# Attention and a two-level expert layer: three moves in the order of the last phases

## The chip, the cores and the metric

The kernel runs on one core of one Trainium2 chip. Its time is the device time in microseconds; three runs of the kernel before took 474.42, 475.54 and 475.85 us, with a median of 475.54. A profiled execution, from which all durations below are taken, spans 474.8 us from the first to the last instruction.

## The reference

Two computations follow each other. The first is attention with 16 query heads that share one key and value head, for 8 batches of 384 tokens with head dimension 64. The second is a hierarchical mixture of experts: each of the 3072 tokens takes the best of 4 groups, then the best of that group's 4 experts, and goes through that expert's two matrices only.

```python
scores = scale * q @ k.T                    # per batch and head
attn = softmax(scores) ; x = attn @ v       # x: 3072 tokens x 1024
g_idx = argmax(x @ w_group)                 # 4 groups, softmax weight g_w
e_idx = argmax(x @ w_expert[g_idx])         # 4 experts in it, softmax weight e_w
h = maximum(x @ w1[g_idx, e_idx], 0)
out = (g_w * e_w) * (h @ w2[g_idx, e_idx])
```

## The kernel before

**Blocks.** A block `p` is 128 queries of one batch with all 16 heads; there are 24 of them, three to a batch (`b, st = divmod(p, 3)`). Each has six pieces `j` of 64 keys. `scores` multiplies queries by keys into a PSUM tile and ScalarE takes its exponential (lines 245 to 254); `pre_add` and `fold_keys` sum the exponentials on VectorE; `values` accumulates the output of the block before in one PSUM tile with a single buffer; `weigh` (line 295) divides by the sums on VectorE and lets GpSimd make the bf16 copy `xbf`.

**Order.** The schedule is written out by hand: each engine executes its instructions in program order, and the loop of lines 549 to 617 sets it. TensorE computes the first three scores of block `p`, then in turn values of block `p - 1` and further scores of block `p`.

**Expert units.** Tokens of one batch mostly choose the same expert. From the first 128 tokens of a batch the kernel counts which expert is chosen most (`choose_a`, `counts`, `choose_b`), reads its number into a register and loads that expert's weights through GpSimd's DMA queue. The batch is then computed with it in 14 units: eight first-layer units of eight matmuls (line 416) with a ReLU on ScalarE, and six second-layer units of eight matmuls (line 424) with a scaled copy on ScalarE. `fill(n)` (line 460) issues the next `n` units. The blocks from 4 on run four or five units each at their end; block 4 (`ST + 1`) has three more, ahead of its `pre_add`. All of these short-lived PSUM results go round one pool of three buffers (`side`, line 76).

**Leftovers.** Tokens that did not choose the counted expert are handled at the end. `counts` sums the one-hot choices over tokens with a matmul of ones: line 342 for the first 128 tokens of a batch, line 344 for the whole batch, whose result goes to `gate_c`. For the last two batches one call holds both: batch 7's first tokens and all of batch 6. Its copy in SBUF, tag `cnt1`, has one buffer. `early_pair` (line 511) reads the counts of all batches, finds one pair of batch and expert that is left over, and loads its number into a register of GpSimd, VectorE and SyncE (line 531); `leftover_w1`, called when 92 units have run, loads the pair's first matrix, and `leftover_w2`, at 98 units, the second. After the last block, the tail packs up to 32 tokens of this pair (`rank_of`, `pick`), transposes their batch's activations (`xe`, line 690), and runs them through the two matrices (`px`, `ph`, `py`), ending in one indirect store (line 723).

**The rare case.** If more is left over, or if the softmax without a subtracted maximum could overflow, a block behind a branch runs (line 774). `bound_a` takes the maxima of the squared query and key norms on VectorE, `bound_b` transposes them on TensorE and compares; `rarei` adds the two conditions, and `values_load` at line 683 reads it into a register of every engine, which the branch tests. With these inputs the block does not run.

## Time and profile before

| what | value |
|---|---|
| time, median of three runs | 475.54 us |
| profiled span | 474.8 us |
| TensorE busy (matmuls) | 459.5 us, 97% |
| VectorE busy | 304.7 us, 64% |
| ScalarE busy | 246.8 us, 52% |
| mean granted clock of TensorE | 0.992 |
| data moved by DMA | 74.52 MB, mean 157 GB/s |

In the profile PE is TensorE's matmuls and PEld its weight loads, which overlap them; DVE is VectorE, ACT ScalarE, POOL GpSimd, SP SyncE. A name with a small q, such as PEq, is an engine's sequencer[...]. Brackets behind an instruction give its engine's idle time just before it and what ended it. The granted clock is TensorE's, as a share of full speed. Idle time counts only where the engine that waits holds up the end.

### The profile page before, as it was taken

To read this page: it belongs to the slowest core of one execution; us is meant where nothing else is said; L and a number is where in the kernel's file an instruction comes from. 1 tells how busy PE (TensorE), PEld (TensorE's weight loads), DVE (VectorE), ACT (ScalarE), POOL (GpSimd) and SP (SyncE) were. 2 spreads that over 40 slices of the span, in tenths; PEclk is the share of its full clock that TensorE was granted. 3 is DMA by queue.
4 is the path that set the end of the run, shared out by engine and by line. 5 is a ranking of instruction groups with operands and counts; after the bars stand their busy time and mean duration, and the time that the engine had idled before them with its cause. 6 is when DMAs were issued, how large, how long until landed. Compare 5 with 4: busy or idle time off the path is not lost. (4 is left out here: it accounts for less than half of the span.)

```text
span 474.8 us, 9339 instructions
## 1 busy us (share of the span) xinstructions
PE 459.5 (97%) x3791; PEld 196.8 (41%) x3807; DVE 304.7 (64%) x483; ACT 246.8 (52%) x359; POOL 60.4 (13%) x83
## 2 busy tenths in 40 slices
PE   8999999999999999999999999999999999999892
PEld 6333434433443344433434334433444334434541
DVE  3998868685695477683694685873687755943200
ACT  2966546546456545645465465565465463613231
POOL 1004003000130003000030001200030000340000
PEclk9999999999999999999999999999999999999898
DMA  8788996978499493967699491987849611899961
GB/s 162 91 132 123 216 211 99 218 170 206 73 172 227 167 157 48 204 146 209 116 138 213 159 166 52 193 159 207 159 66 207 179 60 46 134 213 275 266 177 60
DMA packets 152162, 74.52 MB, mean 157 GB/s; under 512 B 120216, under 2 KB 138652, under 8 KB 152112
## 3 DMA queue, kind: packets, MB, share of 16 engines
q0 software_dynamic: 28416, 37.84, 46.7%
q1 hardware_dynamic: 122896, 35.81, 31.9%
q8 instruction: 32, 0.52, 0.4%
q10 hardware_dynamic: 800, 0.20, 0.2%
q14 instruction: 18, 0.15, 0.1%
HBM read 92.62 MB, written 19.01 MB: 235 GB/s over the span
## 5 line engine op out<-in xcount | busy, mean ns | idle before, releaser
L253 ACT ACTIVATE pt<-s 128x1024 f32<-128x1024 f32 x144 | 142.8, 1026 | 63.5 <-PE s L251 61.1
L251 PE MATMUL s<-qT,kT 64*64 64x512 f32 x1152 | 144.3, 597 | 0.3 <-ACT qT L229 0.2
L290 PE MATMUL o<-pt,v 64*64 64x512 f32 x1152 | 141.0, 590 | 0.0
L261 DVE TENSOR_TENSOR presum<-presum,pt 128x1024 f32<-128x1024 f32 x96 | 116.6, 1215 | 14.7 <-ACT pt L253 8.9
L416 PE MATMUL hps<-xbf,w 128*128 128x384 bf16 x512 | 91.3, 330 | 3.0 <-DVE rarei L682 1.8
L424 PE MATMUL yps<-w,hT 128*128 128x512 bf16 x368 | 84.9, 379 | 0.8
L290 PEld LDWEIGHTS o<-pt,v 64*64 64x64 f32 x1152 | 43.4, 133 | 76.6 <-issue 76.5
L259 DVE TENSOR_TENSOR presum<-pt 128x1024 f32<-128x1024 f32 x24 | 29.1, 1211 | 65.6 <-ACT pt L253 64.9
L416 PEld LDWEIGHTS <-w 128*128 128x128 bf16 x512 | 48.8, 100 | 47.6 <-issue 19.0
L425 ACT ACTIVATE y<-yps,gsel 128x512 f32<-128x512 f32 x48 | 33.0, 687 | 67.3 <-PE yps L424 63.7
L251 PEld LDWEIGHTS s<-qT,kT 64*64 64x64 f32 x1152 | 39.0, 133 | 65.6 <-issue 52.7
L417 ACT ACTIVATE hT<-hps 128x384 bf16<-128x384 f32 x64 | 31.2, 488 | 61.4 <-PE hps L416 55.4
L302 POOL CAST xbf<-xT 128x1024 bf16<-128x1024 f32 x24 | 25.0, 1041 | 299.0 <-DVE xT L301 299.0
L424 PEld LDWEIGHTS <-hT 128*128 128x128 bf16 x384 | 36.5, 98 | 50.3 <-issue 8.5
L145 POOL DMA_DIRECT2D w<-in_moe_w_dram x36 | 24.8, 708 | 68.9 <-issue 43.2
L301 DVE TENSOR_TENSOR xT<-o,rinv 128x1024 f32<-128x1024 f32 x24 | 29.2, 1215 | 4.2 <-PE o L290 4.2
L280 DVE STREAM_TRANSPOSE rinv<-rc 128x1024 f32<-128x1024 f32 x24 | 29.9, 1246 | 0.8
L265 DVE TRANSPOSE_TENSOR_REDUCE fold<-presum 128x32 f32<-128x1024 f32 x24 | 29.6, 1232 | 0.0
L368 DVE COPY L<-lps 128x20 f32<-128x20 f32 (+1 forms) x16 | 3.0, 186 | 34.5 <-PE lps L321 34.5
L243 DVE STREAM_TRANSPOSE qT<-qraw 128x1024 f32<-128x1024 f32 x20 | 24.5, 1225 | 0.6
L209 ACT ACTIVATE qraw<-qraw 128x1024 f32<-128x1024 f32 x21 | 22.0, 1049 | 0.0
L273 PEld LDWEIGHTS sm<-fold,sel 64*64 64x64 f32 x192 | 7.2, 133 | 13.0 <-issue 13.0
(146 smaller groups left out, 167.3 us busy)
## 6 DMA issues: line engine op xcount, KB each, us to landing
w<-in_moe_w_dram POOLq DMA_DIRECT2D x36, 512.0 KB, 10.0
w<-in_moe_w_dram POOLq DMA_DIRECT2D x9, 2048.0 KB, 22.1
out_dram<-y SPq DMA_DIRECT2D x24, 512.0 KB, 3.5
qraw<-in_q_dram SPq DMA_DIRECT2D x56, 192.0 KB, 3.8
x_bf<-xbf SPq DMA_DIRECT2D x8, 768.0 KB, 4.4
v<-in_v_dram SPq DMA_DIRECT2D x16, 96.0 KB, 2.9
k<-in_k_dram SPq DMA_DIRECT2D x28, 48.0 KB, 2.7
qn<-in_q_dram SPq DMA_DIRECT2D x4, 256.0 KB, 4.5
```

The lines of the kernel that those rows point to most:

```text
L251: nc.tensor.matmul(out=ps[64 * c:64 * c + 64, a, :], lhsT=kT[b][r, j * D:(j + 1) * D], rhs=qT[p][r, c * CW:(c + 1) * CW], start=True, stop ...
L253: nc.scalar.activation(out=t[:], in_=ps[:], func=ACTF.Exp, scale=scale)
L259: nc.vector.tensor_add(out=presum[p][:], in0=pt[p, 0][:], in1=pt[p, 1][:])
L261: nc.vector.tensor_add(out=presum[p][:], in0=presum[p][:], in1=pt[p, j][:])
L265: nc.vector.tensor_reduce(out=fold[p][:], in_=presum[p][:].rearrange("p a (n i) -> p (a n) i", i=32), axis=AX, op=OP.add, apply_transpose= ...
L280: nc.vector.transpose(out=t[:].rearrange("p (b i) -> p b i", i=32), in_=rc[:].rearrange("p c b -> p (c b)").unsqueeze(2).to_broadcast([P, ...
L290: nc.tensor.matmul(out=o_ps[p][64 * a:64 * a + 64, c, :], lhsT=v_sb[b][r, j, :], rhs=pt[p, j][r, a, :], start=(j == 0), stop=(j == KB - 1))
L301: nc.vector.tensor_mul(out=xT[b][:, :, ts], in0=o_ps[p][:].rearrange("p c (h n) -> p (c h) n", n=P), in1=rinv[p][:].rearrange("p (h n) -> ...
L416: nc.tensor.matmul(out=ps[:, 0:S], lhsT=w1[:, ko, fc * P:(fc + 1) * P], rhs=xb[:, ko, :], start=(ko == 0), stop=(ko == KO - 1))
L417: nc.scalar.activation(out=state["h"][:, fc, :], in_=ps[:, 0:S], func=ACTF.Relu)
L424: nc.tensor.matmul(out=ps[:], lhsT=state["h"][:, fo, st * P:(st + 1) * P], rhs=w2[:, fo, nh * CW:(nh + 1) * CW], start=(fo == 0), stop=(fo ...
L425: nc.scalar.activation(out=y, in_=ps[:], func=ACTF.Copy, scale=gs_of()[:, st:st + 1])
```

## The change

Four things are altered. The register load of `rare` goes from directly behind `rarei` to a place in front of the last expert unit. `bound_a` goes in front of the units of the last block and `bound_b` behind them, where before they stood behind its second and third unit. The counts of batch 6 leave block 22 for the first unit of block 23, `early_pair` follows them there, and `cnt1` gets a second buffer so that the counts of batch 7's first tokens are kept meanwhile. The three additional units of block 4 go from behind its third scores to behind its fourth, which the first values of block 3 precede.

```diff
 def counts(now, full):
-        t = pool.tile([P, n], FP32, tag="cnt1", bufs=1, name="cnt1")
+        t = pool.tile([P, n], FP32, tag="cnt1", bufs=2, name="cnt1")
...
         if jobs:
             jobs.pop(0)()
-        if p == ST + 1:
-            fill(3)
         for j in (1, 2):
             pre_add(p, j)
         for j in range(KB):
...
             if jobs:
                 jobs.pop(0)()
+            if p == ST + 1 and j == 0:
+                fill(3)
...
             n = 5 if p in FIVES else 4
             steps = {}
+            if p == NP - 1:
+                bound_a()
             if st == 2:
                 steps = {0 if b == 1 else 1: lambda: counts(None, b - 1)}
                 if p == NP - 1:
-                    steps = {1: bound_a, 2: bound_b}
+                    steps = {0: lambda: (counts(None, b - 1), early_pair()), n - 1: bound_b}
             if st == 1:
                 gate_a_, gate_b_ = jobs_gates(b)
-                steps = {n - 3: gate_a_, n - 2: gate_b_, n - 1: lambda: counts(b, b - 1 if b == B - 1 else None)}
+                steps = {n - 3: gate_a_, n - 2: gate_b_, n - 1: lambda: counts(b, None)}
             for i in range(n):
                 fill(1)
                 if i in steps:
                     steps[i]()
-        if p == NP - 2:
-            early_pair()
...
     nc.vector.tensor_copy(out=rarei[:], in_=raref[:, 0:1])
-    rare = nc.values_load(rarei[0:1, 0:1], min_val=0, max_val=2, skip_runtime_bounds_check_because="a sum of two comparisons")
     fill(2)
...
         fill(1)
-    while begun[0] < B or units:
-        fill(1)
+    fill(len(units) - 1)
+    rare = nc.values_load(rarei[0:1, 0:1], min_val=0, max_val=2, skip_runtime_bounds_check_because="a sum of two comparisons")
+    fill(1)
     px = side([P, KO, CAP], FP32, "px")
```

## The prediction

> **What bounds the kernel now.** I read the page first, then TensorE's waits alone, then the order of time around the three places that the diff touches, and last the granted clock microsecond by microsecond.

> The page gives busy shares and instruction counts by engine; the second line is the total of the costliest group of first-layer expert matmuls, with the idle time ahead of it.

> ```profile
> PE 459.5 (97%) x3791; PEld 196.8 (41%) x3807; DVE 304.7 (64%) x483; ACT 246.8 (52%) x359; POOL 60.4 (13%) x83
> ...
> L416 PE MATMUL hps<-xbf,w 128*128 128x384 bf16 x512 | 91.3, 330 | 3.0 <-DVE rarei L682 1.8
> ```

> TensorE is busy 97% of 474.8 us: a microsecond of its waiting is a microsecond of the kernel. The page's chain holds only the final indirect store, so it can't show this; TensorE's own list of waits can (engine, line, who was waited for, total, times, longest):

> ```profile
> PE hps L416 <- DVE rarei L682: 1.8, 1, 1.8
> ...
> PE pq L498 <- DVE sq L492: 0.7, 1, 0.7
> PE hps L416 <- POOL xbf L302: 0.6, 1, 0.6
> ...
> PE cps L344 <- DVE ohe L382: 0.5, 1, 0.5
> ```

> Each wait belongs to an edit: `rarei` to the register load, `sq` to the bound's transpose, `xbf` to block 4's units, `ohe` to the counts that the diff pulls apart. In order of time (start, length, engine and line, idle before it):

> ```profile
> 54.31 3.90 PE L416 MATMUL hps<-xbf,w 128*128 128x384 bf16 x23 [0.62 <-POOL xbf L302]
> ...
> 401.55 0.17 PE L342 MATMUL cps<-ohe,ones_bf 128*128 128x16 bf16 x1
> 402.19 0.18 PE L344 MATMUL cps<-ohe,ones_bf 128*128 128x48 bf16 x1 [0.46 <-DVE ohe L382]
> 402.30 2.81 PE L251 MATMUL s<-qT,kT 64*64 64x512 f32 x24
> ...
> 417.62 0.38 PE L498 MATMUL pq<-ident,sq 128*1 128x128 f32 x2 [0.66 <-DVE sq L492]
> ...
> 440.47 0.73 PE L667 MATMUL pg<-gi,pick 128*128 128x2 f32 x6
> 442.98 4.44 PE L416 MATMUL hps<-xbf,w 128*128 128x384 bf16 x16 [1.78 <-DVE rarei L682]
> ```

> The last line shows more than its wait: sixteen matmuls take 4.44 us, where sixteen take 2.76 at 437.88. The clock says why (stretch, length, busy time and count of PE, PEld, DVE, ACT, POOL, then granted clock, DMA share, GB/s):

> ```profile
> 443.00:444.00 1.00, 1.00 (x5) 0.58 (x5) 0.00 (x0) 0.00 (x0) 0.00 (x0) 0.71 1.08 329
> 444.00:445.00 1.00, 1.00 (x5) 0.44 (x3) 0.00 (x0) 0.00 (x0) 0.00 (x0) 0.50 1.22 221
> 445.00:446.00 1.00, 1.00 (x4) 0.44 (x3) 0.00 (x0) 0.49 (x1) 0.00 (x0) 0.50 1.25 211
> ```

> After the wait TensorE runs about 3 us at half clock. The wait is paid twice.

> [...] TensorE's sequencer passed line 667's semaphore instruction at 439.2, its weights loaded at 440.31; VectorE's register load of line 531 began at 406.6 beside the operation of line 530 (406.60 to 406.83). [...] the 768 KB of `xe` took 8.5 us from issue to landing, the eight stores of the same size 4.4 in the median.

> **The change part by part.** Sums are made from start to start against the profiled span of 474.8 us, then carried to the median of 475.54, 0.74 above it.

> *1. Block 4's three units, behind its fourth scores.* The scores start at 50.93; the same 24 f32 matmuls ahead of units elsewhere take 2.69 (410.19 to 412.88), so the units could start at 53.62 and start at 54.31: 0.69 lost to the xbf cast, which ends at 53.21 + 1.04 = 54.25. Moved, the units stand behind eight value and eight score matmuls (0.86 each) and start at 55.3, past the cast. The values write the output accumulator, free when line 301 ends (51.94 + 1.22 = 53.16); the fourth scores need the first scores' buffer, read by 53.0; each unit needs the exponential of two scores earlier, the third that of the fourth scores (about 56.5) at 57.9. The three ReLUs now follow the fourth exponential on ScalarE, with no DMA in them. No wait in exchange: gain 0.69, bounds 0.3 and 0.7.

> *2. Counts of block 22, `early_pair`, and the second cnt1 buffer.* The first count still runs at 401.55, but the second (line 344) no longer stands between it and the next scores: 402.30 - 401.55 = 0.75 becomes 0.11, as in block 4 (73.63 to 73.74). There the 24 scores then took 2.84 to the first values, against 2.63 here (402.30 to 404.93), because one waits for the count copy behind a ReLU; I charge that 0.21. Gain 0.43. The moved count costs 0.03 in block 23 (85.85 to 85.88); its `ohe` is long ready. The buffer costs 256 bytes a partition and no time; it lets `seen` outlive the next count. `early_pair` and its three register loads (0.48 SP, 0.55 DVE, 0.29 POOL) move. SP: nothing stands behind its load between 406 and block 7's x store at 427.20. POOL: the cast at 416.32 now goes ahead of its load.

> *3. bound_a ahead of the units, bound_b behind them.* Block 23's start of units to its `sm` takes 412.88 to 419.22 = 6.34. Without waiting: four units at 1.30 (449.00 less 447.70), two transposes 0.21 (417.62 to 417.83), 0.11 of changeover and 0.03 for the count: 5.55. Gain 0.79, if `sq` is ready. With `early_pair` gone from its front, VectorE starts this block's sums near 404.3, not 407.25, and is then paced by exponentials; I get fold done at 415.1, `sq` at 415.4, and TensorE's transposes at 417.2. Behind it VectorE runs gate_c (1.1), `early_pair` (2.3), its load, and bound_b (0.9): until about 420.1, then rc and rinv until 421.7. The last values end near 422.9, so weigh isn't delayed. The transpose's PSUM buffer is free by 420, wanted at 424.6. Leftover w1 now needs that register: issue near 419.3 against 419.60 now.

> *4. The register load in front of the last unit.* TensorE gets no `rarei` wait: line 667 starts at 440.47, six such f32 matmuls need 0.58 (399.67 to 400.25), so the units start at 441.05 relative to today's clock, not 442.98: 1.93. Half clock: the two units take 447.25 - 442.98 = 4.27 against 2.60: 1.67. Together 3.60. At the new place TensorE's load (486 ns here) is bounded by 0 and 0.49; the value is ready 15 us earlier, and the sequencer was seen 1.1 us ahead, so I take 0. The other four loads (0.30 SP, 0.46 ACT, 0.31 POOL, 0.33 DVE): ACT has about 1 us idle between evacuations, VectorE is idle before px, POOL before its final store, and SP's last store is issued only when its evacuation ends.

> Sum: 0.69 + 0.43 + 0.79 + 3.60 = 5.5; span 469.3, median 475.54 - 5.5 = 470.0.

> **What an earlier TensorE may run into.** Last w1 piece: issued near 421.6, 25.1 us, landing 446.7, wanted at 464.13 - 5.5 = 458.6. Leftover w2: 437.51 + 19.9 = 457.4, wanted at 460.8. Both hold even if the DMA backlog keeps them where they are. Tightest is `xe`: issued at 434.60, landed at 443.1, first transposed at 447.09. All this moves 1.9 earlier by parts 1 to 3, but the transpose another 3.6: 441.6 against a landing at 441.2. Margin 0.4.

> **The rivals.**
> - The half clock is no stable cost: if the runs that make the median don't pay it, or another place pays it after the change, 1.67 falls away: 471.7. For: [...] a spread of 1.4 us in three runs. Against: nothing else in the last 100 us idles TensorE over 0.7 us before the end.
> - `xe` becomes the new wait by about 1 us: 471.0. For: the margin of 0.4 and a saturated DMA (share above 1 until 455). Against: `xe` keeps its neighbours, as its stores move with it.
> - TensorE's load stalls at its new place: 470.5. Against: the sequencer's lead.
> - Parts 1 to 3 give nothing: 471.9. Against: three waits with one named cause each.
> - Slower: `xe` lands far later than TensorE wants it. A wait over about 1.8 us also brings back 1.67 of half clock, so the gain is gone when `xe` lands at 441.6 + 5.5 - 1.67 = 445.4, a transfer of 12.7 us instead of 8.5. With a landing at 448: 475.54 - 5.5 + 6.4 + 1.7 = 478.1. Against: no transfer through SP's queue in this stretch took over 8.5.

> **How the numbers follow.** Mine 0.60 (alone 469.3 to 470.8), clock 0.14, `xe` 0.13, load 0.05, nothing from parts 1 to 3 0.02, gain just cancelled 0.02, slower 0.04. A difference under 0.3% (1.4 us) can't be told from none. Faster 0.94, same 0.02, slower 0.04. The range 468.9 to 472.2 takes in all the cases that end faster, and 0.4 below my own for charges that don't come (0.21) and spread.

> **What would show it.** Right: no waits of TensorE on `rarei`, `sq`, `xbf`, or on `ohe` at line 344; granted clock 1.00 through the tail; two units after line 667 in 2.6 us; no gap over 0.1 ahead of the last unit's eight matmuls. Wrong: a wait ahead of line 690 with no compute engine to name; a clock of 0.50 before the last matmul; a gap of about half a microsecond at the last unit; `pq` still waiting for `sq`, which would mean VectorE's sums were not paced as I have it.

## The result, and the profile after

The changed kernel takes 470.57 us (median of four runs, 469.97 to 471.02), the kernel before 475.7 (four runs). The ratio is 0.9893 with an interval of 0.9867 to 0.992: 5.1 us, or 1.1%, faster. The profiled span is 468.4 us, 1.6 below that execution's own time of 469.97.

The page, engines and the same group of expert matmuls as before:

```profile
PE 457.0 (98%) x3791; PEld 195.5 (42%) x3807; DVE 304.6 (65%) x483; ACT 246.9 (53%) x360; POOL 60.4 (13%) x83
...
L416 PE MATMUL hps<-xbf,w 128*128 128x384 bf16 x512 | 89.5, 326 | 0.6 <-ACT hT L417 0.6
```

The number of matmuls is the same, but they are busy for 2.5 us less, 1.8 of it in this group. Nearly all of the 1.8 is the half clock, which was booked as work: sixteen matmuls took 4.44 us before and take 2.76 now. TensorE's list of waits:

```profile
PE warm L152 <- DVE one L158: 1.3, 1, 1.3
PE hps L416 <- ACT hT L417: 0.6, 1, 0.6
PE ph L707 <- DVE xc L701: 0.5, 1, 0.5
PE phT L712 <- ACT hg L709: 0.5, 1, 0.5
PE py L719 <- DVEq L774: 0.4, 1, 0.4
PE s L251 <- ACT qT L229: 0.2, 1, 0.2
```

All four waits that the edits addressed are gone and no new one has come; what is left was there before. In order of time, TensorE at the edited places (start, length, count):

```profile
50.43 2.75 PE L251 MATMUL s<-qT,kT 64*64 64x512 f32 x24
...
54.83 4.08 PE L416 MATMUL hps<-xbf,w 128*128 128x384 bf16 x24
58.84 1.09 PE L290 MATMUL o<-pt,v 64*64 64x512 f32 x8
...
400.37 0.17 PE L342 MATMUL cps<-ohe,ones_bf 128*128 128x16 bf16 x1
400.47 3.02 PE L251 MATMUL s<-qT,kT 64*64 64x512 f32 x24
403.31 1.04 PE L290 MATMUL o<-pt,v 64*64 64x512 f32 x8
...
411.27 1.47 PE L416 MATMUL hps<-xbf,w 128*128 128x384 bf16 x8
...
416.50 0.38 PE L498 MATMUL pq<-ident,sq 128*1 128x128 f32 x2
416.82 0.30 PE L273 MATMUL sm<-fold,sel 64*64 64x16 f32 x8
...
438.06 0.73 PE L666 MATMUL pg<-gi,pick 128*128 128x2 f32 x6
438.65 2.76 PE L416 MATMUL hps<-xbf,w 128*128 128x384 bf16 x16
441.25 0.61 PE L688 MATMUL pb<-ident_bf,xe 128*128 128x128 bf16 x8
...
460.33 1.06 PE L719 MATMUL py<-w,hc 128*32 128x256 bf16 x32 [0.38 <-DVEq L774]
```

At the edited places no bracket names a releaser any more. The points of the profile before that the next table needs:

```profile
60.06 1.04 PE L290 MATMUL o<-pt,v 64*64 64x512 f32 x8
...
404.93 0.61 PE L290 MATMUL o<-pt,v 64*64 64x512 f32 x4
...
412.88 4.07 PE L416 MATMUL hps<-xbf,w 128*128 128x384 bf16 x24
...
419.22 0.30 PE L273 MATMUL sm<-fold,sel 64*64 64x16 f32 x8
...
447.25 0.61 PE L690 MATMUL pb<-ident_bf,xe 128*128 128x128 bf16 x8
...
466.34 1.06 PE L720 MATMUL py<-w,hc 128*32 128x256 bf16 x32 [0.38 <-DVEq L775]
```

The profile after is 0.5 us ahead before any edit (block 4's scores at 50.43 instead of 50.93), so I compare distances inside each profile:

| distance | before | after | gain | forecast |
|---|---|---|---|---|
| block 4, first scores to second values | 9.13 | 8.41 | 0.72 | 0.69 |
| the count at the end of block 22 to the first values in block 23 | 3.38 | 2.94 | 0.44 | 0.43 |
| block 23, units to `sm` | 6.34 | 5.55 | 0.79 | 0.79 |
| line 667 (666) to the first transpose of `xe` | 6.78 | 3.19 | 3.59 | 3.60 |
| that transpose to `py` | 19.09 | 19.08 | 0.01 | 0 |

The sum is 5.5. The two spans, 474.8 and 468.4, differ by 6.4: the rest is the 0.5 us ahead of any edit and 0.4 behind `py`, which starts 8.46 us before the end of the profile before and 8.07 before the end of the one after. The register load itself, at its new place (engine queue, minimum, median, maximum in ns, start):

```profile
L694 PEldq TENSOR_LOAD <-rarei x1: 487/487/487, 451.3 to 451.3; - x1
```

It takes 487 ns at 451.3, while the last unit, for which it stands in the program, starts near 455.1 (`px` at 456.85 less one unit of 1.73). TensorE's sequencer is 3.8 us ahead of its array there, and the load costs no time.

### The profile page after: what moved, and what is told of

It is laid out like the page before. It is cut to its first block, busy times and chain, and to the rows that moved or that the text cites. A ratio compares the mean times of both kernels' runs of the same rounds, so it can differ in the third digit from the quotient of the medians.

```text
span 468.4 us, 9356 instructions
## 1 busy us (share of the span) xinstructions
PE 457.0 (98%) x3791; PEld 195.5 (42%) x3807; DVE 304.6 (65%) x483; ACT 246.9 (53%) x360; POOL 60.4 (13%) x83
## 5 line engine op out<-in xcount | busy, mean ns | idle before, releaser
L251 PE MATMUL s<-qT,kT 64*64 64x512 f32 x1152 | 144.6, 597 | 0.3 <-ACT qT L229 0.2
L416 PE MATMUL hps<-xbf,w 128*128 128x384 bf16 x512 | 89.5, 326 | 0.6 <-ACT hT L417 0.6
L416 PEld LDWEIGHTS <-w 128*128 128x128 bf16 x512 | 48.0, 99 | 44.1 <-issue 14.8
L251 PEld LDWEIGHTS s<-qT,kT 64*64 64x64 f32 x1152 | 38.9, 133 | 65.5 <-issue 52.6
L302 POOL CAST xbf<-xT 128x1024 bf16<-128x1024 f32 x24 | 25.0, 1041 | 294.7 <-DVE xT L301 294.7
```

Source lines behind the costliest of these rows:

```text
L251: nc.tensor.matmul(out=ps[64 * c:64 * c + 64, a, :], lhsT=kT[b][r, j * D:(j + 1) * D], rhs=qT[p][r, c * CW:(c + 1) * CW], start=True, stop ...
L416: nc.tensor.matmul(out=ps[:, 0:S], lhsT=w1[:, ko, fc * P:(fc + 1) * P], rhs=xb[:, ko, :], start=(ko == 0), stop=(ko == KO - 1))
```

## The experiments

### One part at a time

The register load alone:

```diff
-    rare = nc.values_load(rarei[0:1, 0:1], ...)
     fill(2)
...
-    while begun[0] < B or units:
-        fill(1)
+    fill(len(units) - 1)
+    rare = nc.values_load(rarei[0:1, 0:1], ...)
+    fill(1)
```

> The kernel before, with the register load of the rare case alone moved to the front of the last unit. My account: TensorE's wait on rarei (1.93 us from start to start) and the half clock behind it (1.67) both go, so line 667 to the first transpose takes about 3.2 us instead of 6.8, and the time falls by 3.6 us (475.7 to about 472.1). Rival, the half clock comes from something else in the tail (the DMA peak, the narrow f32 matmuls): the wait goes, a stretch at clock 0.50 stays, the fall is 1.9 us (473.8). Rival, the load stalls TensorE at its new place: a gap of 0.5 us ahead of the last unit, the fall 3.1 us.

Measured: 472.36 us, ratio 0.9942 (0.9926 to 0.9959). Line 667 at 439.93 to the first transpose at 443.12 is 3.19 us, the clock is 1.00 up to the last matmul, and no gap precedes the last unit. In the trace the first account holds and both rivals fall. The time fell less than the 3.6 us forecast: the medians lie 3.3 apart, and the ratio stands for 2.8 (2.0 to 3.5).

Block 4's units alone:

```diff
-        if p == ST + 1:
-            fill(3)
...
+            if p == ST + 1 and j == 0:
+                fill(3)
```

> The kernel before, with block 4's three units alone moved behind its fourth scores. My account: the wait on xbf goes and nothing takes its place; from block 4's first scores (start) to its second values is 8.4 us instead of 9.1, and all that follows is 0.7 us earlier; in the time that is 0.15%, below what the runs tell apart, so the trace decides. Rival, something later takes the 0.7 us back (a DMA or a buffer): block 22 starts no earlier after block 4's start than before.

Measured: 475.43 us, ratio 1.0003 (0.9985 to 1.0021), which tells nothing, as expected. In the trace first scores to second values take 8.41 us (51.07 to 59.48). Block 22's count comes 349.95 us after those scores (401.02), where it was 350.62 (401.55 less 50.93): the 0.7 us are still there 350 us later.

The counts, `early_pair` and the bound alone (the change with the two other edits undone):

> The changed kernel with block 4's units and the register load put back where they were before: only the counts, early_pair and the bound's two halves are moved. My account: the waits on ohe and sq go, block 22's first count to the first values takes 2.9 us instead of 3.4, block 23's units 5.55 instead of 6.34, together 1.2 us (475.7 to 474.5); the wait on rarei and the half clock stay at about 1.9 and 1.7 us. Rival, the later early_pair gives it back as a wait in the last block's weigh or the leftover weights: no fall, and a new wait of TensorE in the tail.

Measured: 473.69 us, ratio 0.9968 (0.9955 to 0.9981). The first count to the values takes 2.94 us (400.98 to 403.92), block 23's units 5.54 (411.88 to 417.42), and of the waits that the edits address only those on `xbf` and `rarei` are left. Half clock follows the latter as before (sixteen matmuls in 4.30 us). VectorE's later `early_pair` costs nothing. The medians lie 1.9 us apart, more than the 1.2 expected, but the half clock seems to be in fewer executions here, which the table below takes up.

### Where the half clock comes from

The load moved by one unit only:

```diff
-    rare = nc.values_load(rarei[0:1, 0:1], ...)
-    fill(2)
+    fill(1)
+    rare = nc.values_load(rarei[0:1, 0:1], ...)
+    fill(1)
```

> The kernel before, with the register load moved by one unit only, between the two units that followed it. My account, the half clock comes from the length of the idle stretch: one unit fills 1.3 us of the wait, some 0.6 us of idle time stays in front of the second unit, and the clock stays at 1.00; the fall is 1.93 - 0.6 + 1.67 = 3.0 us (475.7 to 472.7). Rival, any wait of TensorE's sequencer on the register load brings the half clock: 0.50 for some 3 us behind the shorter wait, the fall only 1.3 us (474.4).

Measured: 472.77 us, ratio 0.9954 (0.9939 to 0.9969). TensorE's two units behind line 667:

```profile
440.83 1.46 PE L416 MATMUL hps<-xbf,w 128*128 128x384 bf16 x8
442.75 1.46 PE L416 MATMUL hps<-xbf,w 128*128 128x384 bf16 x8 [0.46 <-PE hps L416]
```

The gap is 442.75 - 440.83 - 1.30 = 0.62 us, the second unit runs at full clock, and the medians lie 2.9 us apart. In the trace, moving the load past a single unit leaves 0.62 of the 3.59 us that the whole move brings, so it brings four fifths. It also shows the load's price where it isn't hidden: 0.48 of the 0.62 (the load takes 484 ns, from 442.2 on).

But the times of the kernel before fell into two groups. Over all experiments (the last included, so some more than the expectations below speak of), 88 of 128 executions had a mean clock of 0.994 or less and a median of 475.98 us, the other 40 had 0.996 or 0.997 and 473.91. The half clock is not in every execution. To see what decides, I put waits of several lengths and kinds into the tail. First the late `xe` in the changed kernel, which is also the prediction's slower rival at a small dose:

```diff
-    nc.sync.dma_start(out=xe[:]..., in_=xb_dram[...])
...
     fill(2)
+    nc.sync.dma_start(out=xe[:]..., in_=xb_dram[...])
     pg = side([P, CW], FP32, "pg")
```

> The changed kernel, with the load of xe issued behind the output store that it precedes there, some 3.2 us later (435.4 instead of 432.2). It tests the rival of the prediction (xe as the new wait) and where the half clock comes from: this wait has no register load in it. My account: xe lands at 443.5 to 444.4, TensorE wants it at 441.1, so it waits 2.4 to 3.3 us ahead of the first transpose, and in most runs half clock follows for 3.4 us, another 1.5 us or so: 470.6 becomes 474 to 475.5[...]. Rival, the half clock belongs to the register load or to what is near it: the wait only, clock 1.00 behind it, 473 to 474. Rival, xe had slack enough: no change.

Measured: 473.28 us, ratio 0.9961 (0.9949 to 0.9973). `xe` was issued at 435.8 and took 8.3 us; TensorE waits 2.59 us ahead of line 688 (2.75 from start to start):

```profile
PE pb L688 <- DMA xe<-x_bf: 2.6, 1, 2.6
...
444.00:445.00 1.00, 0.82 (x11) 0.69 (x12) 0.16 (x1) 0.00 (x0) 0.00 (x0) 1.00 1.23 210
445.00:446.00 1.00, 1.00 (x9) 0.61 (x8) 0.53 (x1) 0.00 (x0) 0.00 (x0) 1.00 1.17 214
```

(The first line is from the waits, the others from the table by stretches: clock third from the right.) So `xe` was indeed the next thing to bind, but the longer wait has clock 1.00 behind it, and only five of 22 executions form a slower group (473.91 to 474.68). The account by length alone missed here.

Two differences to the wait on `rarei` were tried apart: that one is a register load, and it follows the six narrow matmuls of line 667, of two columns each. A wait by data at its old place, without a register load (one narrow matmul that needs a chain of VectorE copies; its result is unused), in the changed kernel:

```diff
     nc.vector.tensor_copy(out=rarei[:], in_=raref[:, 0:1])
...
+    nc.vector.tensor_copy(out=hold[:, 0:2], in_=gc[:])
+    nc.vector.tensor_copy(out=hold[:, 2:4], in_=hold[:, 0:2])
...
+    nc.vector.tensor_copy(out=holdb[:], in_=hold[:, 2:4])
...
+    nc.tensor.matmul(out=ph_[:, 0:2], lhsT=ones_bf[:], rhs=holdb[:], start=True, stop=True)
     fill(2)
```

> The changed kernel, with a wait of about 1.9 us put back where the register load stood, but without a register load: one narrow matmul (its result is not used) that needs the result of three VectorE copies behind rarei. It asks why the longer wait of the late xe (2.75 us) brought half clock in few runs. Account A, a TensorE stalled in its sequencer on a register load[...] counts as idle[...]: clock 1.00 behind the wait in nearly all runs, one group near 470.6 + 1.9 = 472.5. Account B, the narrow matmuls of line 667 ahead of the wait count as idle with it, whatever the wait is for: half clock in about two runs of three, as with the kernel before, two groups near 472.5 and 474.4.

Measured: 472.65 us, five executions, none with half clock. And the register load one unit later, behind dense matmuls, with small copies ahead of `rarei`, in the kernel before:

```diff
...
+    nc.vector.tensor_copy(out=hold[:, 0:1], in_=raref[:, 0:1])
+    for i in range(6):
+        nc.vector.tensor_copy(out=hold[:, i + 1:i + 2], in_=hold[:, i:i + 1])
...
-    nc.vector.tensor_copy(out=rarei[:], in_=raref[:, 0:1])
+    nc.vector.tensor_copy(out=rarei[:], in_=hold[:, 6:7])
+    fill(1)
     rare = nc.values_load(rarei[0:1, 0:1], ...)
-    fill(2)
+    fill(1)
```

> The kernel before, with its register load one unit later (as in the run with the load moved by one unit) and seven small VectorE copies of 0.18 us ahead of rarei, so that TensorE waits the same 1.9 us on the register load, but behind eight dense matmuls instead of behind the narrow ones of line 667. Account A (a stall on the register load is what counts as idle): half clock in about two runs of three, two groups near 473.9 and 476, as with the kernel before. Account B (the narrow matmuls count): half clock in few runs, one group near 474.

Measured: 474.31 us, seven executions in one group. Neither the register load nor the narrow matmuls alone brought it in these twelve executions. Both were then lengthened (`range(10)` for the load, five middle copies for the data wait):

> The register load behind one dense unit as in the run before, with four more copies ahead of rarei: the wait is about 2.5 us instead of 1.8, as long as the narrow matmuls and the wait together in the kernel before (2.51). Account C: time with no matmul queued and time of the narrow matmuls add up[...]: two runs of three, two groups near 475.0 and 476.7. Account D: the register load brings half clock only directly behind the narrow matmuls: one group near 475.0, clock 1.00 behind the wait.

> The matmul that waits by data behind the narrow matmuls of line 667, with four more copies ahead of it: the wait is about 2.5 us instead of 1.8, narrow matmuls and wait together 3.2 us. Account C or D[...]: clock 1.00 in nearly all runs, one group near 473.3. Account E: any wait counts, only the length decides and the shorter one fell just under it: half clock in most runs, 475.

Measured: 475.22 us for the load, five of 14 executions in a slower group (476.18 to 476.39); 474.38 us for the data wait, 13 of 15 with a mean clock of 0.993 or less, and half clock in the profiled one:

```profile
441.40 0.18 PE L689 MATMUL hold_ps<-holdb,ones_bf 128*128 128x2 bf16 x1 [2.58 <-DVE holdb L687]
441.44 4.44 PE L416 MATMUL hps<-xbf,w 128*128 128x384 bf16 x16
```

Sixteen matmuls in 4.44 us, the very figure of the kernel before, behind a wait without any register load. The shorter data wait once more, and one a step longer:

> The same kernel as the shorter data wait behind the narrow matmuls (1.9 us, with them 2.5), for more executions: five showed no half clock, where the register load with a stretch as long shows it in 79 of 116 executions of the kernel before. If the kind of wait decides at this length: none or nearly none again, one group near 472.5. If it was chance: half clock in a third or more, a second group near 474.3.

> The same with one copy more: the wait is about 2.1 us, with the narrow matmuls 2.7. If the length decides, between the none of five at 2.5 and the most of fifteen at 3.3: a quarter to two thirds of the executions at half clock, groups near 472.8 and 474.5.

Measured: 472.77 us, with half clock in one or two of six executions (473.45 at clock 0.993, perhaps 473.1 at 0.994), of which the profiled one is one; and 473.54 us, four of seven (473.54 to 473.82).

The traces point to what decides. In the profile before, the clock falls at 443.42, and it falls again when TensorE has finished and the last store is under way:

```profile
470.00:471.00 1.00, 0.00 (x0) 0.00 (x0) 0.00 (x0) 0.00 (x0) 0.00 (x0) 0.86 0.21 54
```

| what TensorE does | wait, start to start | most in one window | half clock in that profile | executions with mean clock of 0.993 or less |
|---|---|---|---|---|
| load one unit later, behind dense matmuls | 0.62 | 1.20 | no | 1 of 15 |
| data (`xe`) behind dense | 2.75 | 1.38 | no | 8 of 22 |
| load behind dense, longest | 2.54 | 1.61 | no | 6 of 14 |
| data behind narrow | 1.91 | 1.65 | no | none of 5 |
| load behind dense | 1.84 | 1.88 | no | none of 7 |
| data behind narrow, one copy more | 2.12 | 1.90 | no | 4 of 7 |
| load behind narrow (block 4's units alone) | 1.92 | 2.14 | yes | 12 of 14 |
| data behind narrow, once more | 1.91 | 2.26 | yes | 1 of 6 |
| load behind narrow (counts and bound alone) | 1.92 | 2.37 | yes | 11 of 22 |
| load behind narrow (kernel before) | 1.93 | 2.51 | yes | 87 of 128 |
| data behind narrow, longest | 2.73 | 2.74 | yes | 13 of 15 |

In these eleven executions the split is clean: 2.14 us or more in one window had half clock, 1.90 or less had none. The late `xe`, with 2.75 us that by this count lay in two windows, 1.37 and 1.38, was spared. This is read from one profile of each kernel; no experiment moved a wait against the window. A register load is not needed. Whether the narrow matmuls count is not shown: without them the same split reads 1.91 against 1.90.

The last column is less sure. A mean clock also falls behind the last matmul, where it costs nothing (in the changed kernel's profile the last matmul ends at 461.39 and the clock falls at 462.86): one of four executions of the changed kernel and three of six of the experiment below have 0.993 or less, though no profile of theirs has half clock before that. By time alone, five executions stand apart in the second row and five in the third. Still, length counts: of the data waits behind narrow matmuls, 1 of 11, 4 of 7 and 13 of 15. The same register load comes with 12 of 14, 87 of 128 and 11 of 22 in kernels that differ at this wait only in when it comes, so shares of unlike kernels don't show that one kind of wait is worse than another; that stays open.

### A version beyond the change

The `px` matmuls go in front of the last unit, so that VectorE's copy of their result runs beside it:

```diff
     fill(len(units) - 1)
     rare = nc.values_load(rarei[0:1, 0:1], ...)
-    fill(1)
     px = side([P, KO, CAP], FP32, "px")
...
     nc.vector.tensor_copy(out=xc[:], in_=px[:])
+    fill(1)
```

> The changed kernel, with the px matmuls in front of the last unit instead of behind it, and the register load in front of them, so that VectorE's copy of px runs beside the last unit. My account: the gap of 0.52 us ahead of ph goes and the chain to the last store is 0.5 us shorter (470.6 to 470.1), too little for the runs to tell, so the trace decides. Rival: the last unit's output store now comes too close to the final indirect store, which waits for it: nothing gained.

Measured: 470.35 us, ratio to the kernel before 0.9903 (0.9875 to 0.9932), not to be told from the change itself. The end of it:

```profile
459.75 1.06 PE L719 MATMUL py<-w,hc 128*32 128x256 bf16 x32 [0.38 <-DVEq L774]
460.86 0.47 ACT L721 ACTIVATE yc<-py,gc 128x256 f32<-128x256 f32 x1 [1.83 <-PE py L719]
462.92 1.09 POOL L722 DMA_INDIRECT out_dram<-yc,rows  x1 [26.93 <-POOLq L774]
```

`py` is 0.58 us earlier than in the changed kernel (460.33), but the final store starts at 462.92, 1.6 us after the copy ahead of it ends, instead of at 462.20. The last unit's output store was issued at 458.4 and lands 3.3 us later, at 461.7, after the copy. That the final store waits for it fits the rival; the trace doesn't name it. In the changed kernel this output store lands at 460.7, before the copy ends at 461.9.

## Why the prediction was right

**Parts 1 to 3.** Each wait had one named cause, the moved work stood beside other work as it was priced, and the gains came to within 0.03 us. (The 24 matmuls from 410.19 to 412.88, by which the prediction priced block 4's scores, are value matmuls of the same size.) `sq` was early enough (done at 414.4, its transposes at 416.50); VectorE's longer queue behind it didn't delay the last `weigh`, for which VectorE itself waited 1.94 us on TensorE.

**Part 4.** Wait and half clock together were sized to 0.01 us for the profiled execution, and the load at its new place costs nothing. The ground for taking 0 out of 0 to 0.49 was the 1.1 us by which the sequencer had been seen ahead at line 667; at the new place it is 3.8 us ahead.

**From the profile to the median.** This step was weaker, and the number owes something to luck. The 5.5 us were measured in an execution with half clock that took 476.45 us, and were subtracted whole from a median of 475.54. The half clock is paid in 88 of 128 executions only, so the average over executions can fall by 5.5 less 1.67 x 40 / 128, which is 5.0. The rival of the unstable clock was right in that; it had been given as all or nothing. Measured were 5.1, with an interval of 3.8 to 6.3, which can't tell 5.0 from 5.5. The register load alone shows the same: 1.93 + 1.67 x 88 / 128 is 3.1, where 3.6 was expected and 2.8 (by the ratio) or 3.3 (by the medians) came. That two of the first three executions were of the slower group was luck: from a median in the faster one, 473.91, the same sum gives 468.4, 2.2 below what was measured.

**The start.** The two groups lie 2.07 us apart, 0.4 more than the two units lose in the profile. The start differs between executions as well. The 18 warm-up matmuls of line 451 last 314 ns each in the profile before, 2.13 us in all; in the one after they last 314 down to 219, 1.63 in all, and the first query transposes (line 228) start at 6.80 and 6.31, which is the 0.5 us by which the profile after is ahead. In the profiles of the first four experiments the warm-up takes 1.46, 2.13, 1.55 and 1.93 us and the transposes start at 6.14, 6.95, 6.24 and 6.61: the later the longer it takes. Whether the windows set this is not shown, and how it adds up to the 0.4 wasn't worked out.

**`xe`.** The margin was put at 0.4 us; it was 0.8 (issue at 432.19, 8.1 us to landing, weights loaded at 441.08). The experiment agrees: issued 3.6 us later, `xe` made TensorE wait 2.75. The slower outcome would have needed 12.7 us from issue to landing, and `xe` took 8.1 to 8.3. Its term that a wait over 1.8 us brings back the half clock was too simple, since these 2.75 mostly did not.

## What to carry to other kernels

Put a register load that every engine executes where its value has long been ready and its slowest reader's sequencer is well ahead (3.8 us here); one unit of work in between brought four fifths of it here. Look at what follows a wait as well: matmuls that take longer than usual (here sixteen in 4.44 us instead of 2.76) are a second bill for the same wait, and busy shares hide it. Before carrying a profiled loss to a median, see in how many executions it occurs, and which of them was profiled.

## What the runs showed of the hardware

- The half clock lasted 3.4 us. A microsecond at a mean clock of 0.71 holds 0.42 us at full clock and 0.58 at half; read so from the table by stretches, it runs from 443.42 to 446.82 in the kernel before and from 442.22 to 445.62 in the third experiment. In four profiles the clock fell twice, 27.30 to 27.32 us apart, which is eight times 3.41, and the first fall came at another time in each: 443.42, 443.72, 442.22 and 442.06.
- The clock fell without 3.4 us of idling: in the kernel before, the stretch from 440.00 to the fall at 443.42 held 2.51 us of narrow matmuls and waiting and 0.9 us of dense matmuls. Behind the late `xe`, a wait of 2.75 us that by the estimate above lay in two windows, it stayed at 1.00.
- A register load took 0.48 us on TensorE when exposed (with the load moved by one unit only), and with the sequencer 3.8 us ahead, in the changed kernel, it cost no time.
